# Masking half the key chunks on GpSimd after the exp, and moving three wide expert tiles

## The chip, the cores and the metric

The kernel runs on one core of one Trainium2 chip. The metric is the device time of one execution in microseconds; before the change the median of three runs is 723.05 us (722.39 to 724.26). The engines of a core run side by side and meet at semaphores: TensorE (PE) multiplies matrices, VectorE (DVE) and ScalarE (ACT) do elementwise work, GpSimd (POOL) does elementwise work and gathers, SyncE (SP) issues most transfers.

## The reference

Block-sparse attention over 4 batches of 8 heads, 768 positions, head size 64, in blocks of 32; then one expert of eight per token.

```python
scores = scale * np.matmul(q, k.transpose(0, 1, 3, 2))
mask = np.abs(blk_i - blk_j) <= 1                       # neighbouring blocks
mask |= (blk_i == 0) | (blk_j == 0) | (blk_i == n_blocks - 1) | (blk_j == n_blocks - 1)
for qb in range(n_blocks):
    for kb in sampled_blocks[qb]:                       # three random blocks for each
        mask[qb*32:(qb+1)*32, kb*32:(kb+1)*32] = True
scores = np.where(mask, scores, -1e9)
attn = softmax(scores)                                  # cut: minus max, exp, sum + 1e-9
x = (attn @ v)                                          # rows of 512: one per token, 3072 tokens
logits = x @ w_gate
expert_idx = argmax(logits); gate_w = softmax(logits)[expert_idx]
y = relu(x @ w1[expert_idx]) @ w2[expert_idx]           # w1: 512x1024, w2: 1024x512 for each expert
return gate_w[:, None] * y
```

The mask is the same for every head.

## The kernel before

Two stages. The attention goes through 16 pairs of heads (four batches of four pairs), each in two halves of 384 queries. Keys stand in six chunks of 128 on the partitions. For each chunk the scores of both heads go to one PSUM tile, ScalarE takes the exp, VectorE adds the six exps for the denominators, TensorE multiplies with v. There are three PSUM buffers for scores (`ps_s`, used by transposes too), and eight slots for exps (`ea`).

The mask is added to the scores by a second matmul into the same PSUM: `oh` (one-hot of a key's block) times `pen` (0 where a query sees the block, -2^33 where not), both bf16.

```python
def e_slot(n, half, c):
    return ea[:, ((2 * n + half) * NCH + c) % 8, :].rearrange("p (h q) -> p h q", h=2)

def scores(n, half, c):
    ...
    s = upper["ps_s"].tile([P, 2, 512], F32, name="s")
    for hh in range(2):
        r = slice(hh * D, (hh + 1) * D)
        nc.tensor.matmul(s[:, hh, :CW], lhsT=kT[r, c * P : (c + 1) * P], rhs=qT[r, cols], start=True, stop=False)   # L237
    for hh in range(2):
        r = slice(hh * D, (hh + 1) * D)
        nc.tensor.matmul(s[:, hh, :CW], lhsT=oh[r, c, :], rhs=pen[r, cols], start=False, stop=True)                 # L240
    e = e_slot(n, half, c)
    nc.scalar.activation(e, s[:, :, :CW], AF.Exp, scale=scale)                                                      # L242
    es[(n, half, c)] = e
    if c == 1:
        esums[(n, half)] = work.tile([P, 2, CW], F32, name="esum")
    if c > 0:
        t = esums[(n, half)]
        nc.vector.tensor_add(t[:], es[(n, half, 0)] if c == 1 else t[:], e)                                         # L248

def attend(n, half, c):
    ...
    for hh in range(2):
        nc.tensor.matmul(
            op[hh * D : (hh + 1) * D, :], lhsT=v_sb[:, hh, c, :], rhs=e[:, hh, :], start=(c == 0), stop=(c == NCH - 1),
        )                                                                                                           # L258
    ...

def divide(n, half):
    ...                                                             # sp: sums over keys, by TensorE, L271; ss: its copy
    for m in range(HC):
        nc.vector.reciprocal(r[:, m * P : (m + 1) * P], ss[:, m * P : (m + 1) * P])                                 # L278
    nc.vector.tensor_mul(oT[:], oT[:], r[:])                                                                        # L279

steps = [(n, half) for n in range(len(pairs)) for half in range(2)]
for i, (n, half) in enumerate(steps):
    ...
    if 0 < i and n + 1 < len(pairs):
        turn(*pairs[n + 1], half)                                   # tp: transposes of the next pair's k or q, L217
    for c in range(NCH):
        scores(n, half, c)
    if i == 0:
        make_mix()
    if i == 10:
        route_consts()                                              # small constants, on GpSimd
    if i > 0:
        divide(*steps[i - 1])
    for c in range(NCH):
        attend(n, half, c)
    if i == 0:
        turn(*pairs[1], 0)
    if n > 0:
        rows_out(n - 1, half)                                       # xr: rows of x and logits, L291; gate(b) at a batch's end
```

PE, DVE and POOL run their instructions in this order. `gate(b)` takes the softmax of a batch's logits and has one exp on ScalarE.

The experts' stage goes through 19 tiles of 128 tokens of one expert (`layer1`, L806; `layer2`, L820). For what is left of an expert there are three units (up to 224 tokens, L924 and L932) and three small tiles (32 tokens); unit u and small tile u stand behind tile `AT[u]`. Each tile, unit and small tile loads its expert's w1 and w2, 2 MB each, into two buffers for w1 and two for w2.

```python
AT = (8, 11, 14)
AT_S = (8, 11, 14)
...
for i in range(NS):
    ...
    if i + 3 in AT:
        gather_u(AT.index(i + 3))
    if i + 3 in AT_S:
        gather_s(AT_S.index(i + 3))
    if i + 2 in AT:
        turn_u()
    ...
    if i + 1 in AT:
        ...                                                         # layer 2 of tile i, the unit, layer 2 of tile i + 1
        layers_u(u, P + more * STEP, banks)
```

Of the kernel before, what the change touches and what calls it, by code (L numbers as in the profile page):

```python
# [17 lines left out]
def kernel(  # L18
# [30 lines left out]
    QR = 3 * P // 4  # L49
    STEP = P // 8  # L50
    MW = P + QR
    AT = (8, 11, 14)
    KU = len(AT)

    QS = P // 4
    AT_S = (8, 11, 14)
    KS = len(AT_S)
    NS = KA - -(N - KA * P - KU * MW - KS * QS) // P
    NTB = NC - KA
    NB_ = NTB + 2 * KU + KS  # L60
    assert KA < AT[0] - 2 and all(b - a > 2 for a, b in zip(AT, AT[1:])) and AT_S == AT and AT[-1] < NS - 3
    assert TA * P - E * (P - 1) > (KA - 1) * P
    XW = DM + 8
    scale = 1.0 / float(D) ** 0.5
# [56 lines left out]

    oh = mpool.tile([P, NCH, P], BF16, name="oh")
    pen = mpool.tile([P, S], BF16, name="pen")

    mix = mpool.tile([P, NPR, P + E], F32, name="mix")
    ones = mpool.tile([P, D], F32, name="ones")
# [61 lines left out]
    def make_mix():  # L188
        nc.scalar.dma_start(wg[:], moe_w_gate.rearrange("(c p) e -> p c e", p=P))
        nc.gpsimd.memset(mix[:], 0.0)  # L190
        for pr in range(NPR):
            nc.gpsimd.tensor_copy(mix[:, pr, :P], ident[:])
            nc.gpsimd.tensor_copy(mix[:, pr, P:], wg[:, pr, :])

    make_mask_pool = ExitStack()
    by_hand = ExitStack()
    by_hand.enter_context(tc.manual_schedule(engines={mybir.EngineType.Pool, mybir.EngineType.PE, mybir.EngineType.DVE}))
# [31 lines left out]
    def scores(n, half, c):  # L229

        b, pr = pairs[n]
        kT, qT = turned[(b, pr)][0], turned[(b, pr)][1]
        cols = slice(half * CW, (half + 1) * CW)
        s = upper["ps_s"].tile([P, 2, 512], F32, name="s")
        for hh in range(2):
            r = slice(hh * D, (hh + 1) * D)
            nc.tensor.matmul(s[:, hh, :CW], lhsT=kT[r, c * P : (c + 1) * P], rhs=qT[r, cols], start=True, stop=False)  # L237
        for hh in range(2):
            r = slice(hh * D, (hh + 1) * D)
            nc.tensor.matmul(s[:, hh, :CW], lhsT=oh[r, c, :], rhs=pen[r, cols], start=False, stop=True)  # L240
        e = e_slot(n, half, c)
        nc.scalar.activation(e, s[:, :, :CW], AF.Exp, scale=scale)  # L242
        es[(n, half, c)] = e
        if c == 1:
            esums[(n, half)] = work.tile([P, 2, CW], F32, name="esum")
        if c > 0:
            t = esums[(n, half)]
            nc.vector.tensor_add(t[:], es[(n, half, 0)] if c == 1 else t[:], e)  # L248

    def attend(n, half, c):  # L250
        v_sb = loaded[pairs[n]][2]
        if c == 0:

            ops_[(n, half)] = rt["bank"] = ps_o.tile([P, 512], F32, name="op")
        op = ops_[(n, half)][:, :CW]
        e = es[(n, half, c)]
        for hh in range(2):
            nc.tensor.matmul(  # L258
                op[hh * D : (hh + 1) * D, :], lhsT=v_sb[:, hh, c, :], rhs=e[:, hh, :], start=(c == 0), stop=(c == NCH - 1),
            )  # L260
        if c == NCH - 1:
            oT = work.tile([P, CW], F32, name="oT", bufs=3)
            nc.scalar.copy(oT[:], op)  # L263
            ops_[(n, half)] = oT
# [13 lines left out]
            nc.vector.reciprocal(r[:, m * P : (m + 1) * P], ss[:, m * P : (m + 1) * P])  # L278
        nc.vector.tensor_mul(oT[:], oT[:], r[:])  # L279

    def rows_out(n, half):

        b, pr = pairs[n]
        oT = ops_.pop((n, half))
        M = P + E
        xr = ps_x.tile([P, HC, M], F32, name="xr")

        M_ = D if n + 1 < len(pairs) else P
        for m in range(HC):
            for j in range(P // M_):  # L290
                nc.tensor.matmul(  # L291
                    xr[j * M_ : (j + 1) * M_, m, :], lhsT=oT[:, m * P + j * M_ : m * P + (j + 1) * M_], rhs=mix[:, pr, :],
                    start=True, stop=True,
                )
        if half == 0:
            xbs[n] = xpool.tile([P, NCH, M], F32, name="xb")
        xb = xbs[n]
        ms = slice(half * HC, (half + 1) * HC)
        nc.scalar.copy(xb[:, ms, :], xr[:])
        sofar = lgn[:, b * NCH + half * HC : b * NCH + (half + 1) * HC, :]  # L300
        if pr == 0:
            nc.vector.tensor_copy(sofar, xb[:, ms, P:])
        else:
            nc.vector.tensor_add(sofar, sofar, xb[:, ms, P:])
        if half == 1:
            rows = x_d[b * S : (b + 1) * S, pr * P : (pr + 1) * P]
            nc.sync.dma_start(rows.rearrange("(p c) w -> p c w", p=P), xb[:, :, :P])
            if pr == NPR - 1:
                gate(b)

    def gate(b):
        ts = slice(b * NCH, (b + 1) * NCH)
        nc.vector.reduce_max(lmax[:, ts], lgn[:, ts, :], axis=AX)
        ge = small.tile([P, NCH, E], F32, name="ge", bufs=2)
        nc.vector.tensor_tensor(
            ge[:], lgn[:, ts, :], lmax[:, ts].unsqueeze(2).to_broadcast([P, NCH, E]), op=ALU.subtract,
        )
        nc.scalar.activation(ge[:], ge[:], AF.Exp)
        gs = small.tile([P, NCH], F32, name="gs", bufs=2)
        nc.vector.reduce_sum(gs[:], ge[:], axis=AX)  # L320
        nc.vector.tensor_scalar_add(gs[:], gs[:], 1e-9)
        nc.vector.reciprocal(gs[:], gs[:])
        gw = small.tile([P, NCH, XW - DM], F32, name="gw", bufs=2)
        nc.vector.tensor_copy(gw[:], gs[:].unsqueeze(2).to_broadcast([P, NCH, XW - DM]))
        nc.sync.dma_start(x_d[b * S : (b + 1) * S, DM:].rearrange("(p c) w -> p c w", p=P), gw[:])

    pairs = [(b, pr) for b in range(B) for pr in range(NPR)]

    def shifted(n, half):

# [33 lines left out]
    def attention_again():  # L364
        for n in range(len(pairs)):
            load(*pairs[n])
            for which in range(2):
                turn(*pairs[n], which)
            for half in range(2):
                shifted(n, half)  # L370
                for c in range(NCH):
                    attend(n, half, c)
                divide(n, half)
                rows_out(n, half)

    def judge():

# [295 lines left out]
    def one_hots_1(ph, sl, T, n):  # L673
        sl_i = sm.tile([P, T], I32, name="sl_i" + ph)
        nc.vector.tensor_copy(sl_i[:], sl[:])
        rc_i = sm.tile([P, 2, T], I32, name="rc_i" + ph)
        nc.vector.tensor_scalar(rc_i[:, 0, :], sl_i[:], scalar1=P - 1, scalar2=None, op0=ALU.bitwise_and)
        nc.vector.tensor_scalar(rc_i[:, 1, :], sl_i[:], scalar1=7, scalar2=None, op0=ALU.arith_shift_right)
        rc = rt["rc" + ph] = sm.tile([P, 2, T], F32, name="rc" + ph)
        nc.vector.tensor_copy(rc[:], rc_i[:])  # L680
        oc = sm.tile([P, T, n], BF16, name="oc" + ph)
        nc.vector.tensor_tensor(
            oc[:], rt["iota_r"][:, None, :n].to_broadcast([P, T, n]), rc[:, 1, :].unsqueeze(2).to_broadcast([P, T, n]),
            op=ALU.is_equal,
        )
        tk = rt["tk" + ph] = sm.tile([P, T, 2, n], BF16, name="tk" + ph)
        for j in range(2):
            nc.vector.tensor_tensor(  # L688
                tk[:, :, j, :], oc[:], rt["tok"][:, j, :T].unsqueeze(2).to_broadcast([P, T, n]), op=ALU.mult,
            )  # L690
        rt["or" + ph] = sm.tile([P, T, P], BF16, name="or" + ph)

    def tokens(ph, T, n):

# [258 lines left out]


    steps = [(n, half) for n in range(len(pairs)) for half in range(2)]
    NA = (B - 1) * NPR
    load(*pairs[1])
    for i, (n, half) in enumerate(steps):
        if half == 1 and n + 2 < len(pairs):
            load(*pairs[n + 2])  # L960
        if 0 < i and n + 1 < len(pairs):
            turn(*pairs[n + 1], half)
        for c in range(NCH):
            scores(n, half, c)
        if i == 0:
            make_mix()
        if i == 10:
            route_consts()
        if i > 0:
            divide(*steps[i - 1])  # L970
        for c in range(NCH):
            attend(n, half, c)
        if i == 0:
            turn(*pairs[1], 0)
        if n > 0:
            rows_out(n - 1, half)

        if (n, half) == (NA, 1):
            ranks("A", 0, TA)
        if (n, half) == (NA + 1, 0):  # L980
            count("A")
            layout_a()
            for i_ in range(2):
                fetch(i_, 1)
                fetch(i_, 2)
        if (n, half) == (NA + 1, 1):
            slots_a()
        if n == NA + 2:
            one_hots("A", rt["slA"], TA, KA, half)
        if (n, half) == (NA + 3, 0):  # L990
            tokens("A", TA, KA)
            for i_ in range(3):
                gather(i_)
        if n + 1 == len(pairs) and half == 1:
            turn_x(0)
# [6 lines left out]
    for i in range(NS):  # L1002
# [58 lines left out]
        if i == 1:  # L1061
            tokens("B", NT, NB_)
        if i == 2:
            judge()
        if i == 4:
            tokens_s()
        if i == 3:
            for u in range(KU):
                at = rt["xeU"][0:1, KU + u : KU + u + 1]
# [96 lines left out]
```

## Time and profile before

The profiled execution has a span of 722.3 us. One half of a pair is about 10.8 us, and the attention takes the first 355 us; the experts' stage takes the rest.

| engine | busy us | share of the span | instructions |
|---|---|---|---|
| TensorE | 701.8 | 97% | 5134 |
| VectorE | 393.6 | 54% | 825 |
| ScalarE | 281.2 | 39% | 456 |
| GpSimd | 72.6 | 10% | 114 |

An average over both stages hides that their limits differ: VectorE is busy 70 to 80% of most of the attention and little later, the transfers are the other way round (25% to 36% of the DMA engines' time in most of the attention, mostly 88% and more from 370 us on). In the lines that follow, a line of the order of time has start, length, engine, line of the kernel, operation, output and inputs, shape, and number of instructions put together; in square brackets stands the idle time before it. A line of a group has count, busy time and mean length, then the idle time before it and who ended it. One matmul of f32 stands as two records.

### The profile page before, as it was taken

What the parts mean: (1) busy time and instruction counts of PE and PEld (TensorE: products, weight loads), DVE (VectorE), ACT (ScalarE), POOL (GpSimd) and SP (SyncE); (2) the same over time, 40 slices, a digit from 0 to 9 for tenths busy, and PEclk for the clock granted to TensorE, in tenths of its full rate; (3) what the DMA queues carried; (4) which work ended last, traced back from release to release, by engine and by line L of the source; (5) the groups of instructions that cost most, each with busy time, mean ns of one, the idle gap of its engine ahead of it and who ended that gap; (6) DMA issues with size and microseconds to landing.
All of it is one profiled execution on the core that took longest, in us unless ns stands there. A gap on an engine that the chain in (4) does not pass through costs nothing.

```text
span 722.3 us, 13053 instructions
## 1 busy us (share of the span) xinstructions
PE 701.8 (97%) x5134; PEld 457.6 (63%) x5134; DVE 393.6 (54%) x825; ACT 281.2 (39%) x456; POOL 72.6 (10%) x114
## 2 busy tenths in 40 slices
PE   8999999999999999999999999999999999899993
PEld 5555555555555555555677776778787868677861
DVE  6677778678678678999748025820227011902200
ACT  3756756756756766765411110111111111111110
POOL 7000000000000000000202112201130013011210
PEclk9999999999999999999999999999999999999998
DMA  9312323322333322193278899996999399979950
GB/s 198 88 50 62 88 74 84 89 60 51 89 81 76 88 65 47 47 382 129 82 256 289 309 321 362 360 333 222 378 395 370 147 364 396 399 237 384 397 188 18
DMA packets 114566, 145.48 MB, mean 201 GB/s; under 512 B 56227, under 2 KB 72675, under 8 KB 114468
## 3 DMA queue, kind: packets, MB, share of 16 engines
q1 hardware_dynamic: 107968, 129.84, 54.1%
q0 software_dynamic: 4368, 14.02, 5.1%
q8 instruction: 51, 0.84, 0.5%
q10 hardware_dynamic: 2132, 0.41, 0.3%
q14 instruction: 47, 0.39, 0.2%
HBM read 131.47 MB, written 12.94 MB: 200 GB/s over the span
## 4 chain that ended last, share of the span: by engine, by line
PE 57%; issue 33%; POOL 4%; DVE 3%; DMA 1%; POOLq 0%; ACTq 0%; another core or an unknown queue 0%; DVEq 0%
PE s L237 17%; PE op L258 17%; PE hp L806 6%; PE s L240 4%; PE sp L271 4%; PE xr L291 3%; PE zp L820 3%; PE tp L217 2%; POOL out_dram L835 2%; POOL xg L738 1%; DMA q_sb<-in_q_dram 1%; DVE orB L668 0%; POOL ea L858 0%; POOL ea L903 0%; DVE tkB L688 0%
## 5 line engine op out<-in xcount | busy, mean ns | idle before, releaser
L237 PE MATMUL s<-qT,kT 64*128 64x384 f32 x768 | 157.1, 487 | 1.2 <-DVE qT L222 1.2
L242 ACT ACTIVATE ea<-s 128x768 f32<-128x768 f32 x192 | 152.3, 813 | 6.2 <-PE s L240 4.2
L806 PEld LDWEIGHTS hp<-xgT,w 128*128 128x128 f32 x1216 | 138.3, 192 | 7.8 <-issue 5.1
L806 PE MATMUL hp<-xgT,w 128*128 128x128 f32 x1216 | 140.7, 276 | 1.4 <-ACT hT L813 1.4
L787 DVE STREAM_TRANSPOSE xgT<-xg 32x128 f32<-32x128 f32 x208 | 62.9, 302 | 128.6 <-PE hp L806 98.8
L248 DVE TENSOR_TENSOR esum<-esum,ea 128x768 f32<-128x768 f32 x128 | 122.7, 958 | 13.8 <-ACT ea L242 0.5
L258 PE MATMUL op<-ea,v_sb 128*64 128x384 f32 x768 | 129.3, 486 | 0.0
L820 PE MATMUL zp<-w,hT 128*128 128x512 f32 x256 | 112.7, 594 | 0.0
L258 PEld LDWEIGHTS op<-ea,v_sb 128*64 128x64 f32 x768 | 55.1, 137 | 68.8 <-issue 68.8
L237 PEld LDWEIGHTS s<-qT,kT 64*128 64x128 f32 x768 | 66.4, 187 | 37.6 <-issue 34.4
L278 DVE RECIPROCAL r<-ss 128x128 f32<-128x128 f32 x96 | 82.2, 912 | 1.3 <-ACT ss L273 1.3
L820 PEld LDWEIGHTS zp<-w,hT 128*128 128x128 f32 x256 | 47.5, 190 | 54.6 <-issue 54.6
L813 ACT ACTIVATE hT<-hp 128x512 f32<-128x512 f32 x36 | 21.5, 597 | 114.3 <-PE hp L806 106.4
L248 DVE TENSOR_TENSOR esum<-ea 128x768 f32<-128x768 f32 x32 | 30.7, 958 | 59.8 <-ACT ea L242 59.8
L240 PE MATMUL s<-pen,oh 64*128 64x384 bf16 x384 | 62.9, 322 | 0.0
L263 ACT COPY oT<-op 128x384 f32<-128x384 f32 x32 | 15.3, 479 | 106.2 <-PE op L258 106.2
L825 ACT ACTIVATE zo<-zp,xg 128x512 f32<-128x512 f32 x16 | 11.0, 687 | 101.7 <-PE zp L820 101.7
L913 DVE STREAM_TRANSPOSE ea<-ea 32x128 f32<-32x128 f32 x84 | 21.7, 285 | 29.7 <-DMA ea<-x_rows,gB 29.0
L240 PEld LDWEIGHTS <-oh 64*128 64x128 bf16 x384 | 19.0, 94 | 25.1
L291 PEld LDWEIGHTS xr<-mix,oT 128*64 128x64 f32 (+1 forms) x372 | 24.1, 139 | 10.7 <-issue 10.7
L835 POOL DMA_INDIRECT out_dram<-zo,sB x14 | 14.0, 1004 | 167.2 <-ACT zo L825 119.1
L738 POOL DMA_INDIRECT xg<-x_rows,gA x5 | 6.1, 1224 | 220.7 <-ACT ea L242 219.4
(278 smaller groups left out, 520.2 us busy)
## 6 DMA issues: line engine op xcount, KB each, us to landing
w<-in_moe_w_dram SPq DMA_DIRECT2D x50, 2048.0 KB
k_sb<-in_k_dram SPq DMA_DIRECT2D x32, 192.0 KB
v_sb<-in_v_dram SPq DMA_DIRECT2D x16, 384.0 KB
x_rows<-xb SPq DMA_DIRECT2D x16, 384.0 KB
q_sb<-in_q_dram SPq DMA_DIRECT2D x30, 192.0 KB
sums<-ss SPq DMA_DIRECT2D x32, 3.0 KB
q_sb<-in_q_dram ACTq DMA_DIRECT2D x2, 192.0 KB
xg<-x_rows,gB POOLq DMA_INDIRECT x15, 7.0
```

The costliest lines, as they stand in the source:

```text
L237: nc.tensor.matmul(s[:, hh, :CW], lhsT=kT[r, c * P : (c + 1) * P], rhs=qT[r, cols], start=True, stop=False)
L240: nc.tensor.matmul(s[:, hh, :CW], lhsT=oh[r, c, :], rhs=pen[r, cols], start=False, stop=True)
L242: nc.scalar.activation(e, s[:, :, :CW], AF.Exp, scale=scale)
L248: nc.vector.tensor_add(t[:], es[(n, half, 0)] if c == 1 else t[:], e)
L258: nc.tensor.matmul(op[hh * D : (hh + 1) * D, :], lhsT=v_sb[:, hh, c, :], rhs=e[:, hh, :], start=(c == 0), stop=(c == NCH - 1),)
L271: nc.tensor.matmul(sp[hh * D : (hh + 1) * D, :], lhsT=ones[:], rhs=esum[:, hh, :], start=True, stop=True)
L278: nc.vector.reciprocal(r[:, m * P : (m + 1) * P], ss[:, m * P : (m + 1) * P])
L291: nc.tensor.matmul(xr[j * M_ : (j + 1) * M_, m, :], lhsT=oT[:, m * P + j * M_ : m * P + (j + 1) * M_], rhs=mix[:, pr, :], start=True, stop ...
L787: nc.vector.transpose(xT[d, :, t], xg[t, :DM].rearrange("p (c q) -> p c q", c=DB)[:, :, d])
L806: nc.tensor.matmul(hp[:, m, :], lhsT=st[i]["w1"][:, c, fb * P : (fb + 1) * P], rhs=st[i]["xT"][:, c, :], start=(c == 0), stop=(c == DB - 1),)
L820: nc.tensor.matmul(zp[:], lhsT=st[i]["hT"][:, fb, :], rhs=st[i]["w2"][:, fb, :], start=(fb == 0), stop=(fb == FB - 1),)
L835: ins = nc.gpsimd.indirect_dma_start(out=to[:, :], out_offset=bass.IndirectOffsetOnAxis(ap=at, axis=0), in_=rows, in_offset=None, bounds_c ...
```

## The change

- In pairs 1 to 11 (the first three batches without the first pair) chunks 0, 1 and 2 have no mask matmul. Instead GpSimd multiplies their exps in place with a 0/1 mask in SBUF (bf16, three chunks of 128x768), which is made once behind the first half by six matmuls and three compares.
- The chunks are multiplied with v in the order 3, 0, 4, 1, 5, 2, and VectorE's adds start behind the fourth exp, so that GpSimd has time before a masked chunk is read.
- The exp of `gate(b)` and what follows it come after the next half's products with v; the route constants are made in half 0, since GpSimd is taken later.
- Units and small tiles stand behind tiles 6, 10 and 14, four tiles apart.

```diff
-    AT = (8, 11, 14)
+    AT = (6, 10, 14)
...
-    AT_S = (8, 11, 14)
+    AT_S = (6, 10, 14)
...
+    LATE = (0, 1, 2)
+    ORDER = (3, 0, 4, 1, 5, 2)
+    mask = mpool.tile([P, len(LATE), S], BF16, name="mask")
...
+    def make_late():
+        for j, c in enumerate(LATE):
+            bm = upper["ps_s"].tile([P, 2, 512], F32, name="bm", tag="s")
+            for half in range(2):
+                cols = slice(half * CW, (half + 1) * CW)
+                nc.tensor.matmul(bm[:, half, :CW], lhsT=oh[:D, c, :], rhs=pen[:D, cols], start=True, stop=True)
+            nc.vector.tensor_single_scalar(mask[:, j, :].rearrange("p (h q) -> p h q", h=2), bm[:, :, :CW], 0.0, op=ALU.is_ge)
...
+        late = c in LATE and 0 < n < NA
...
-            nc.tensor.matmul(s[:, hh, :CW], lhsT=kT[r, c * P : (c + 1) * P], rhs=qT[r, cols], start=True, stop=False)
-        for hh in range(2):
+            nc.tensor.matmul(s[:, hh, :CW], lhsT=kT[r, c * P : (c + 1) * P], rhs=qT[r, cols], start=True, stop=late)
+        for hh in range(0 if late else 2):
             r = slice(hh * D, (hh + 1) * D)
             nc.tensor.matmul(s[:, hh, :CW], lhsT=oh[r, c, :], rhs=pen[r, cols], start=False, stop=True)
...
-        if c == 1:
-            esums[(n, half)] = work.tile([P, 2, CW], F32, name="esum")
-        if c > 0:
+        if late:
+            m = mask[:, LATE.index(c), cols]
+            nc.gpsimd.tensor_tensor(e, e, m[:, None, :].to_broadcast([P, 2, CW]), op=ALU.mult)
+        if c >= 3:
+            if c == 3:
+                esums[(n, half)] = work.tile([P, 2, CW], F32, name="esum")
             t = esums[(n, half)]
-            nc.vector.tensor_add(t[:], es[(n, half, 0)] if c == 1 else t[:], e)
+            for c_ in {3: (0,), 4: (4, 1), 5: (5, 2)}[c]:
+                nc.vector.tensor_add(t[:], es[(n, half, 3)] if c == 3 else t[:], es[(n, half, c_)])
...
         if i == 0:
             make_mix()
-        if i == 10:
             route_consts()
         if i > 0:
             divide(*steps[i - 1])
-        for c in range(NCH):
+        for c in ORDER:
             attend(n, half, c)
         if i == 0:
+            make_late()
             turn(*pairs[1], 0)
+        if "gates" in rt:
+            gate_weights(*rt.pop("gates"))
```

Cut: `gate` is split into its first part and `gate_weights`, `tokens_s` comes two tiles earlier, and the one-hot tiles of the two routings share a buffer.

More of the change, by code (lines that the diff above doesn't have):

```diff
@@ L60 @@
     NB_ = NTB + 2 * KU + KS
-    assert KA < AT[0] - 2 and all(b - a > 2 for a, b in zip(AT, AT[1:])) and AT_S == AT and AT[-1] < NS - 3
+    assert KA < AT[0] and all(b - a > 2 for a, b in zip(AT, AT[1:])) and AT_S == AT and AT[-1] < NS - 3
     assert TA * P - E * (P - 1) > (KA - 1) * P
@@ L123 @@
     pen = mpool.tile([P, S], BF16, name="pen")
+    LATE = (0, 1, 2)
+    ORDER = (3, 0, 4, 1, 5, 2)
+    assert NCH == 6
+    mask = mpool.tile([P, len(LATE), S], BF16, name="mask")
     mix = mpool.tile([P, NPR, P + E], F32, name="mix")
@@ L243, in scores @@
         es[(n, half, c)] = e
-        if c == 1:
-            esums[(n, half)] = work.tile([P, 2, CW], F32, name="esum")
-        if c > 0:
+        if late:
[4 more added lines that the diff above has]
+                esums[(n, half)] = work.tile([P, 2, CW], F32, name="esum")
             t = esums[(n, half)]
-            nc.vector.tensor_add(t[:], es[(n, half, 0)] if c == 1 else t[:], e)
+            for c_ in {3: (0,), 4: (4, 1), 5: (5, 2)}[c]:
+                nc.vector.tensor_add(t[:], es[(n, half, 3)] if c == 3 else t[:], es[(n, half, c_)])
     def attend(n, half, c):
         v_sb = loaded[pairs[n]][2]
-        if c == 0:
+        if c == ORDER[0]:
             ops_[(n, half)] = rt["bank"] = ps_o.tile([P, 512], F32, name="op")
@@ L258, in attend @@
             nc.tensor.matmul(
-                op[hh * D : (hh + 1) * D, :], lhsT=v_sb[:, hh, c, :], rhs=e[:, hh, :], start=(c == 0), stop=(c == NCH - 1),
+                op[hh * D : (hh + 1) * D, :], lhsT=v_sb[:, hh, c, :], rhs=e[:, hh, :], start=(c == ORDER[0]), stop=(c == ORDER[-1]),
             )
-        if c == NCH - 1:
+        if c == ORDER[-1]:
             oT = work.tile([P, CW], F32, name="oT", bufs=3)
@@ L279, in divide, with rows_out @@
         nc.vector.tensor_mul(oT[:], oT[:], r[:])
-    def rows_out(n, half):
+    def rows_out(n, half, again=None):
         b, pr = pairs[n]
@@ L308, in rows_out, with gate @@
             if pr == NPR - 1:
-                gate(b)
-    def gate(b):
+                gate(b, again)
+    def gate(b, n_again=None):
         ts = slice(b * NCH, (b + 1) * NCH)
@@ L317, in gate, with gate_weights @@
         )
+        if b < B - 1 and n_again is None:
+            rt["gates"] = (b, ge)
+        else:
+            gate_weights(b, ge)
+    def gate_weights(b, ge):
         nc.scalar.activation(ge[:], ge[:], AF.Exp)
@@ L327 @@
     pairs = [(b, pr) for b in range(B) for pr in range(NPR)]
+    NA = (B - 1) * NPR
     def shifted(n, half):
@@ L370, in attention_again @@
                 shifted(n, half)
-                for c in range(NCH):
+                for c in ORDER:
                     attend(n, half, c)
                 divide(n, half)
-                rows_out(n, half)
+                rows_out(n, half, True)
     def judge():
@@ L690, in one_hots_1 @@
             )
-        rt["or" + ph] = sm.tile([P, T, P], BF16, name="or" + ph)
+        rt["or" + ph] = sm.tile([P, T, P], BF16, name="or" + ph, tag="or")
     def tokens(ph, T, n):
@@ L955 @@
     steps = [(n, half) for n in range(len(pairs)) for half in range(2)]
-    NA = (B - 1) * NPR
     load(*pairs[1])
@@ L970 @@
             divide(*steps[i - 1])
-        for c in range(NCH):
+        for c in ORDER:
             attend(n, half, c)
         if i == 0:
+            make_late()
             turn(*pairs[1], 0)
+        if "gates" in rt:
+            gate_weights(*rt.pop("gates"))
         if n > 0:
@@ L1063 @@
         if i == 2:
+            tokens_s()
             judge()
-        if i == 4:
-            tokens_s()
         if i == 3:
```

## The prediction

> **What bounds the kernel now.** I read the page first: engine shares, then the 40 slices. Columns of the first line are busy us (share of the span) and number of instructions; a digit of the second is the busy tenths of one slice of 18 us.
>
> ```profile
> PE 701.8 (97%) x5134; PEld 457.6 (63%) x5134; DVE 393.6 (54%) x825; ACT 281.2 (39%) x456; POOL 72.6 (10%) x114
> ...
> PE   8999999999999999999999999999999999899993
> ...
> DVE  6677778678678678999748025820227011902200
> ...
> POOL 7000000000000000000202112201130013011210
> ```
>
> TensorE has work from beginning to end, and GpSimd next to none in the attention (slices 2 to 19). A busy matmul row says little by itself, because matmuls overlap; so I went to the order of time on TensorE in one half of a pair (start, length, what):
>
> ```profile
> 153.38 0.81 PE L237 MATMUL s<-qT,kT 64*128 64x384 f32 x4
> 154.03 0.33 PE L240 MATMUL s<-pen,oh 64*128 64x384 bf16 x2
> 154.28 0.87 PE L271 MATMUL sp<-esum,ones 128*64 128x384 f32 x4
> 154.98 4.04 PE L258 MATMUL op<-ea,v_sb 128*64 128x384 f32 x24
> 158.85 0.86 PE L291 MATMUL xr<-mix,oT 128*64 128x136 f32 x12
> 159.65 0.59 PE L217 MATMUL tp<-ident,k_sb 64*128 64x64 f32 x12
> 160.07 0.86 PE L237 MATMUL s<-qT,kT 64*128 64x384 f32 x4
> 160.77 0.33 PE L240 MATMUL s<-pen,oh 64*128 64x384 bf16 x2
> 160.93 0.81 PE L237 MATMUL s<-qT,kT 64*128 64x384 f32 x4
> ```
>
> Starts follow one another without a hole and no line carries an idle time: the attention is paced by TensorE. From the starts, one chunk of scores is 0.65 us of L237 and 0.16 us of L240 (160.77 to 160.93). The two L240 matmuls of a chunk are each 0.33 us long, yet together take the place of 0.16 us. The first exp of a half starts at 150.36 and of the next at 161.14 in ScalarE's order of time, so a half lasts **10.78 us**. Six chunks at 0.81 us, sp 0.70, op 3.87, xr 0.80 and tp 0.42 are 10.65 of it.
>
> In the second stage I asked for TensorE's waits after 340 us (us in total, times, longest):
>
> ```profile
> PE hpu L924 <- DMA w<-in_moe_w_dram: 3.9, 2, 2.3
> PE hp L806 <- ACT hT L813: 1.4, 3, 0.5
> ```
>
> The first are the units behind tiles 11 and 14, whose first weights come 1.65 and 2.25 us late; the unit behind tile 8 waits for nothing.
>
> The other engines, from the groups (busy us, mean ns of one):
>
> ```profile
> L242 ACT ACTIVATE ea<-s 128x768 f32<-128x768 f32 x192 | 152.3, 813 | 6.2 <-PE s L240 4.2
> ...
> L248 DVE TENSOR_TENSOR esum<-esum,ea 128x768 f32<-128x768 f32 x128 | 122.7, 958 | 13.8 <-ACT ea L242 0.5
> ...
> L278 DVE RECIPROCAL r<-ss 128x128 f32<-128x128 f32 x96 | 82.2, 912 | 1.3 <-ACT ss L273 1.3
> ```
>
> A half costs VectorE five adds (4.8), three reciprocals (2.57 by the order of time), one oT product (0.56) and one logit add (0.18), 8.1 us of 10.78. ScalarE has six exps (4.85) and copies, about 7.2. Neither is the bound.
>
> [...] in the first 17 us, in GpSimd's and VectorE's order of time:
>
> ```profile
> 12.99 0.24 POOL L424 TENSOR_SCALAR past<-row 128x1 f32<-128x1 f32 x1
> 13.32 0.19 POOL L425 TENSOR_TENSOR quarter<-quarter,past 128x1 f32<-128x1 f32 x1
> ...
> 14.62 0.97 POOL L425 TENSOR_TENSOR quarter<-quarter,past 128x1 f32<-128x1 f32 x1
> ```
>
> ```profile
> 3.93 2.67 DVE L169 SCALAR_TENSOR_TENSOR allow<-kb,samp,allow 24x24 f32<-24x24 f32 x3
> ...
> 14.58 4.15 DVE L248 TENSOR_TENSOR esum<-esum,ea 128x768 f32<-128x768 f32 x4
> ```
>
> The same one-element GpSimd op takes 0.19 us alone and 0.97 us beside an esum add that started at 14.58; and three 24-element VectorE ops take 0.89 us each while GpSimd's selects of 768 elements (0.86 us each) run. It is a lock, in both directions. [...] No run here shows a long two-input GpSimd op. [...]
>
> **The change part by part.**
>
> 1. *Mask matmuls removed.* Chunks 0, 1, 2 in pairs 1 to 11, two halves: 66 chunks. 66 x 0.16 = **-10.7 us** of TensorE, or 0.48 us a half: TensorE's own pace becomes 10.30 us. TensorE being the bound, this counts in full if nothing else takes over.
>
> 2. *GpSimd products added.* 66 products, 128x768 f32 times a bf16 mask, three a half. [...] TensorE does not wait for them either: in the half above the first exp ends at 151.17, [...] in the order 3, 0, 4, 1, 5, 2 the last masked chunk is read at about 157.7 (154.98 less 0.48 of removed matmuls, plus five chunks of 0.645).
>
> 3. *The lock.* What excludes one another in a half is VectorE's five adds, oT product and logit add, 5 x 0.96 + 0.56 + 0.18 = 5.52 us, and three products of length T: 5.52 + 3T. [...] So the lock equals the old pace at T = 1.75 and frees the new pace of 10.30 only at T below 1.59. Over 22 halves: -10.7 us for T up to 1.59, [...] +16 us at 2.0 (11.52).
>
> 4. *The mask made ahead* (half 0). Six bf16 matmuls and three VectorE compares of 128x768 from PSUM. A 128x384 copy from PSUM takes 0.55 us here (L222), so a compare of twice that is some 0.95. VectorE's five adds now start behind the fourth exp (about 15.2 us) and end near 20.4; compares end near 21.5, 22.5 and 23.5. The three score buffers hold the compares' input, so the next tp, tp and first score matmuls, which stood at 19.81, 20.23 and 20.61, wait one after the other: the first score starts near 23.5. **+2.9 us**.
>
> 5. *Units at 6, 10, 14.* Four tiles, not three, between units. A tile is 14.0 us of TensorE (452.24 to 466.25) and asks for two loads of 2 MB; with a unit and its small tile come four more loads in a burst. After the unit behind 8 the DMA share is 0.92 to 1.04 from 500 to 560 us, a backlog that three tiles don't work off. A fourth adds 14.0 us against two loads at 5.3 us each (the shortest distance between landings, from the packets) and about 1.4 us of gathers and stores: 2 us to spare, as much as the larger wait. Both waits go: **-3.9 us**. Before tile 6 TensorE waits for no load, so an earlier first unit is safe.
>
> 6. *Gates' exp one half later, constants in half 0, adds behind the fourth exp.* TensorE waits for none of these before, and what they do is not on its path: 0.
>
> Sum of 1, 4 and 5 with a free lock: -10.7 + 2.9 - 3.9 = -11.7, or 711. [...]
>
> **The rivals.** *The lock takes over* (T of 1.7 or more): for it, the 0.97 us above [...]. It gives 718 to 740. Against it, [...] one-input GpSimd work here runs at a rate that a two-input loop of 2 reads an element would do in 2 x 0.83 x 768 = 1.28 us plus 0.19, 1.47 us (the copies of 128 and 8 columns, 291 and 192 ns, give 0.83 ns an element). *The late masked chunks stall TensorE through the eight exp buffers*: the fifth add of a half ends later than before, and the fifth exp of the next half writes the buffer it reads. Unblocked there are some 5 us between them, so it only joins in when the lock already binds, and would add 1 to 3 us. *The loads stay late*: the burst, not the spacing, sets them, and the waits only move: 4 us less gain, 715 with a free lock.
>
> **Range and chances.** I take T from 1.45 to 1.8 as about equally likely and weigh the free lock a little more than half, because even 1.47 us follows from this trace's own rates. That puts the middle at 715. The low end is the full sum and a few us of small gains, 709; the high end is T near 1.95, 734. Over 2% faster (below 708.6) needs more than TensorE gives up: 0.06. Over 2% slower (above 737.5) needs T of 2.0 or more: 0.12. Within 2%: 0.82.
>
> **What would show it.** The L255 group (mask matmuls) has 252 rows and not 384. A product's time by itself, when no add stands beside it, should be 1.4 to 1.8 us; adds beside products should be longer than 958 ns by the wait for the lock. The distance of exps between halves should be 10.3 us with a free lock; 10.6 to 11 with holes in TensorE that end on GpSimd or VectorE says the lock binds. The first score of half 1 near 23.5 us shows step 4. No wait for weights before the units shows step 5. It is wrong if TensorE waits for the products though the lock is free, or if a unit behind tile 6 meets loads that have not caught up.

## The result, and the profile after

The changed kernel takes **733.54 us** (median of four runs, 733.36 to 736.21) against 722.96 us: a ratio of **1.0152**, 95% interval 1.0126 to 1.0179. It is 1.5% slower. The prediction was 715 us, 1.1% faster than before, with 709 to 734 as the range: the time is just inside the range, the direction is wrong. That it lies inside is luck: the high end stood for a GpSimd product of about 1.95 us, and the product takes 1.64.

The page of the changed kernel; the same lines as of before:

```profile
PE 697.8 (95%) x5008; PEld 455.3 (62%) x5008; DVE 440.4 (60%) x828; ACT 271.8 (37%) x456; POOL 184.0 (25%) x180
...
PE   8999997999979999999999899999999998999994
...
DVE  5799997999979998899747109302660027402200
...
POOL 6145544445535430000202211021210222011210
```

TensorE is busy 4 us less and the kernel takes 9.5 us longer. TensorE's string has dips in slices 7, 12 and 23 (7, 7 and 8), where it was full before: holes in single places, not a slower pace. VectorE is nearly full in the attention, and GpSimd is at work there now.

The groups of the instructions that the change added or touched (busy us, mean ns), the last two of them first as they were before the change:

```profile
L279 DVE TENSOR_TENSOR oT<-oT,r 128x384 f32<-128x384 f32 x32 | 17.9, 558 | 1.1
L304 DVE TENSOR_TENSOR lgn<-lgn,xb 128x24 f32<-128x24 f32 x24 | 4.4, 182 | 5.8 <-ACT xb L299 5.8
```

```profile
L261 POOL TENSOR_TENSOR ea<-ea,mask 128x768 f32<-128x768 f32 x66 | 115.3, 1775 | 131.7 <-ACT ea L257 118.4 <-DVE r L297 13.2
...
L298 DVE TENSOR_TENSOR oT<-oT,r 128x384 f32<-128x384 f32 x32 | 31.6, 986 | 1.1
...
L323 DVE TENSOR_TENSOR lgn<-lgn,xb 128x24 f32<-128x24 f32 x24 | 23.1, 962 | 5.3 <-ACT xb L318 5.3
```

The lock can be read here although no line names it: a logit add of 24 columns takes 962 ns and took 182 before, an oT product 986 and took 558. That is waiting, written down as work. A GpSimd product takes 1636 ns at the least (the shortest of the 66).

TensorE in an ordinary half of the changed kernel, in order of time:

```profile
161.91 0.59 PE L231 MATMUL tp<-ident,k_sb 64*128 64x64 f32 x12
162.33 2.80 PE L252 MATMUL s<-qT,kT 64*128 64x384 f32 x16
164.97 0.32 PE L255 MATMUL s<-pen,oh 64*128 64x384 bf16 x2
...
166.84 0.87 PE L290 MATMUL sp<-esum,ones 128*64 128x384 f32 x4
167.53 4.04 PE L277 MATMUL op<-ea,v_sb 128*64 128x384 f32 x24
171.40 0.86 PE L310 MATMUL xr<-mix,oT 128*64 128x136 f32 x12
172.20 0.59 PE L231 MATMUL tp<-ident,q_sb 64*128 64x64 f32 x12
```

No hole, and from one tp to the next 10.29 us: the predicted pace, to 0.01 us. So the loss lies elsewhere. TensorE's waits show where (us in total, times, longest):

```profile
PE s L252 <- ACT ea L257: 9.6, 3, 4.4
PE hp L833 <- DMA w<-in_moe_w_dram: 3.9, 2, 2.0
PE okp L417 <- DVE okn L416: 3.3, 2, 2.6
```

The first line stands at the end of each of three batches (4.43, 4.43 and 0.71 us). ScalarE at the first of them:

```profile
105.73 4.51 ACT L257 ACTIVATE ea<-s 128x768 f32<-128x768 f32 x6
...
120.64 0.24 ACT L344 ACTIVATE ge<-ge 128x48 f32<-128x48 f32 x1 [4.53 <-DVE ge L334]
120.79 2.19 ACT L257 ACTIVATE ea<-s 128x768 f32<-128x768 f32 x3
```

and VectorE and TensorE beside it:

```profile
110.21 1.63 DVE L323 TENSOR_TENSOR lgn<-lgn,xb 128x24 f32<-128x24 f32 x1
111.76 0.95 DVE L267 TENSOR_TENSOR esum<-ea 128x768 f32<-128x768 f32 x1
...
120.40 0.21 DVE L334 TENSOR_TENSOR ge<-lgn,lmax 128x48 f32<-128x48 f32 x1
```

```profile
115.05 2.15 PE L252 MATMUL s<-qT,kT 64*128 64x384 f32 x12
121.64 1.65 PE L252 MATMUL s<-qT,kT 64*128 64x384 f32 x4 [4.43 <-ACT ea L257]
```

The exp of the gates is **ahead** of the next half's six exps in ScalarE's queue. The text of the changed kernel has it behind them, but only PE, DVE and POOL keep the order of the text here; ScalarE's is chosen by the scheduler, which took the gates' exp first. It waits 4.53 us for VectorE's `ge`, the exps wait behind it, the three score buffers fill, and TensorE stops after three chunks. Before the change the exp stood ahead of the next exps too, and cost next to nothing there, since VectorE delivered in time:

```profile
107.22 4.85 ACT L242 ACTIVATE ea<-s 128x768 f32<-128x768 f32 x6
...
117.85 0.24 ACT L318 ACTIVATE ge<-ge 128x48 f32<-128x48 f32 x1 [0.24 <-DVE ge L315]
```

In all four batches together it waited 1.4 us before and 11.1 us now.

Where the 9.5 us between the two profiled spans (722.3 and 731.8) come from, by the start of the first exp of each half:

| part | working | us |
|---|---|---|
| mask made ahead | pair 1 starts at 33.68, not 31.76; the first half itself started 0.3 us earlier here | +1.9 |
| pace of 22 halves | 22 x (10.29 - 10.78) | -10.8 |
| two batch ends | (15.06 + 11.63) + (15.06 + 11.78) - 4 x 10.29 | +12.4 |
| third batch end, and the rest of the attention | last half at 349.15, not 344.37, less the lines above | +1.3 |
| experts' stage | 372.75 us behind the last sp matmul, not 367.97 | +4.8 |

The pace paid what it was to pay, and two kinds of wait took more than that. (The parts are rounded; they sum to 9.6.)

### The profile page after: what moved, and what is told of

Read it like the earlier page. It is cut to its first block, busy times and chain, and to the rows that moved or that the text cites. A ratio compares the mean times of both kernels' runs of the same rounds, so it can differ in the third digit from the quotient of the medians.

```text
span 731.8 us, 12893 instructions
## 1 busy us (share of the span) xinstructions
PE 697.8 (95%) x5008; PEld 455.3 (62%) x5008; DVE 440.4 (60%) x828; ACT 271.8 (37%) x456; POOL 184.0 (25%) x180
## 4 chain that ended last, share of the span: by engine, by line
issue 40%; DVE 28%; PE 22%; POOL 4%; DMA 2%; ACT 1%; POOLq 0%; DVEq 0%; ACTq 0%; another core or an unknown queue 0%
DVE esum L267 13%; PE s L252 8%; PE op L277 7%; DVE r L297 6%; DVE lgn L323 2%; POOL out_dram L862 2%; PE hp L833 2%; POOL xg L765 2%; PE sp L290 2%; PE s L255 2%; PE xr L310 1%; ACT ea L257 1%; DVE ea L940 1%; DMA xg<-x_rows,gB 1%; PE tp L231 1%
## 5 line engine op out<-in xcount | busy, mean ns | idle before, releaser
L252 PE MATMUL s<-qT,kT 64*128 64x384 f32 x768 | 149.6, 496 | 10.9 <-ACT ea L257 9.6
L257 ACT ACTIVATE ea<-s 128x768 f32<-128x768 f32 x192 | 146.0, 812 | 9.3 <-PE s L255 6.9
L261 POOL TENSOR_TENSOR ea<-ea,mask 128x768 f32<-128x768 f32 x66 | 115.3, 1775 | 131.7 <-ACT ea L257 118.4
L833 PE MATMUL hp<-xgT,w 128*128 128x128 f32 x1216 | 142.3, 278 | 5.3 <-DMA w<-in_moe_w_dram 3.9
L267 DVE TENSOR_TENSOR esum<-esum,ea 128x768 f32<-128x768 f32 x128 | 126.2, 986 | 12.2 <-ACT ea L257 0.5
L252 PEld LDWEIGHTS s<-qT,kT 64*128 64x128 f32 x768 | 68.4, 190 | 52.5 <-ACT ea L257 28.7
L267 DVE TENSOR_TENSOR esum<-ea 128x768 f32<-128x768 f32 x32 | 37.4, 1169 | 22.2 <-ACT ea L257 22.1
L255 PE MATMUL s<-pen,oh 64*128 64x384 bf16 x252 | 41.7, 326 | 0.0
L298 DVE TENSOR_TENSOR oT<-oT,r 128x384 f32<-128x384 f32 x32 | 31.6, 986 | 1.1
L290 PE MATMUL sp<-esum,ones 128*64 128x384 f32 x128 | 27.7, 512 | 0.0
```

Of the source, the lines that this page charges most:

```text
L261: nc.gpsimd.tensor_tensor(e, e, m[:, None, :].to_broadcast([P, 2, CW]), op=ALU.mult)
L267: nc.vector.tensor_add(t[:], es[(n, half, 3)] if c == 3 else t[:], es[(n, half, c_)])
L290: nc.tensor.matmul(sp[hh * D : (hh + 1) * D, :], lhsT=ones[:], rhs=esum[:, hh, :], start=True, stop=True)
L833: nc.tensor.matmul(hp[:, m, :], lhsT=st[i]["w1"][:, c, fb * P : (fb + 1) * P], rhs=st[i]["xT"][:, c, :], start=(c == 0), stop=(c == DB - 1),)
```

## The experiments

Times are compared with the kernel before on the same chip, whose median in the first four was 724.4 us, in the second four 724.17 and in the last 723.13.

**1. The gates' exp truly behind the next half's exps.**

```diff
-            nc.scalar.copy(oT[:], op)
+            rt["copied"] = nc.scalar.copy(oT[:], op)
...
     def gate_weights(b, ge):
-        nc.scalar.activation(ge[:], ge[:], AF.Exp)
+        with tc.issue_after(getattr(rt["copied"], "ins", rt["copied"])):
+            nc.scalar.activation(ge[:], ge[:], AF.Exp)
```

> The changed kernel with one thing different: on ScalarE the exp of the gates is queued behind the next half's copy of the product with v, and so behind its six exps, where the change put it only in the text. Theory (ScalarE, which runs in order, stands behind the gates' exp, which waits for VectorE): the two halves of 15.06 us become 10.29, the ones after them 10.3 instead of 11.63 and 11.78, the half of 12.16 about 11; 733.5 - 2 x 6.2 - 1 = 720, +-1.5. Rival (VectorE is behind because of the lock with GpSimd, and will catch up with TensorE at some other point): halves beyond 10.3 stay, 728 or more.

Measured: 720.49 us, ratio 0.9941 (0.9921 to 0.9961). From the changed kernel's 1.0152 that is 2.1%, 15 us (the two intervals leave about 2.5 us either way). All halves of pairs 1 to 11 but the last are now 10.29 or 10.30 us, the batch ends too; from the first exp of pair 1 to that of the last half it is 302.07 us instead of 315.47, and the 13.4 us of difference are the two batch ends' 12.4 and 1.0 of the third batch end and the halves behind it. (Pair 1 starts at 35.73 in this profile and not at 33.68, mostly because the first score chunks of the kernel started 1.6 to 1.7 us apart instead of 0.81. Such a start is no part of the change; the kernel of experiment 9 has it too, so halves and stages are compared and not whole spans.) ScalarE's queue shows the mend, in the kernel of experiment 3:

```profile
118.70 3.65 ACT L257 ACTIVATE ea<-s 128x768 f32<-128x768 f32 x5
...
127.02 0.48 ACT L282 COPY oT<-op 128x384 f32<-128x384 f32 x1 [3.14 <-PE op L277]
127.40 0.24 ACT L345 ACTIVATE ge<-ge 128x48 f32<-128x48 f32 x1
```

The rival, that VectorE's lag would come out elsewhere, falls: in most halves VectorE's first add starts 6.0 to 7.0 us behind the half's first exp, where it was mostly 6.0 in the changed kernel. It lags no less, and the halves still keep 10.29.

**2. The health check ahead of the small tiles' row lists.**

```diff
         if i == 2:
-            tokens_s()
             judge()
+            tokens_s()
```

> The changed kernel with one thing different: behind tile 2 the health check (judge) comes ahead of the small tiles' row lists (tokens_s), as it did before the change. Theory (VectorE stands in order behind a result of TensorE for the row lists, TensorE then waits 3.3 us for the health check and runs at half its clock for a while): 3.3 us of wait and 1.6 us of slower matmuls go, 728.5 +-1. Rival (the wait is there because the route lists came late, and moves elsewhere): 732 to 734.

Measured: 730.57 us, ratio 1.0088 (1.007 to 1.0106), 0.64% or 4.6 us below the changed kernel. From the last half's first exp to the end of the profile it is 377.1 us, where it is 382.7 in the changed kernel and 377.9 in the kernel before. The changed kernel's VectorE explains it:

```profile
400.27 0.20 DVE L734 TENSOR_TENSOR sB<-tvB,noneB 128x35 int32<-128x35 f32 x1
414.16 0.16 DVE L742 COPY tvS<-tps 128x3 f32<-128x3 f32 x1 [13.69 <-PE tps L740]
...
416.10 0.55 DVE L416 TENSOR_REDUCE okn<-ok 64x1 f32<-64x384 f32 x1
```

VectorE has nothing to do from 400.5 to 414 because the copy at the head of its queue waits for TensorE, and the sums for the health check, whose inputs are long there, stand behind the copy. When TensorE comes to the check, it has to wait for them:

```profile
416.70 0.19 PE L417 MATMUL okp<-ones,okn 64*1 64x1 f32 x2 [2.58 <-DVE okn L416]
417.64 0.19 PE L417 MATMUL okp<-ones,okn 128*1 128x1 f32 x2 [0.76 <-DVE okn L416]
417.76 5.47 PE L833 MATMUL hp<-xgT,w 128*128 128x128 f32 x32
```

3.34 us of wait, and 32 matmuls that start over 5.31 us and not 3.68, at a granted clock of 0.50 from 418.7 to 420.7 us and of 1.00 from 421.7. In the order of experiment 2 the sums are made by 405.9 us, and TensorE goes through:

```profile
416.81 0.30 PE L417 MATMUL okp<-ones,okn 64*1 64x1 f32 x4
```

**3. Both mends.** The two diffs together.

> Both of the two mends together. Theory: they lie in different stages and add up, 733.5 - 13.4 - 5 = 715 +-2, which is below the kernel before (723). Rival: one of them uncovers another wait, 720 or more.

Measured: **715.49 us, ratio 0.9871 (0.9854 to 0.9888)**: 1.3% faster than the kernel before, and the sum of the two single gains (0.9941 - 0.0064 = 0.9877). This version is faster than both kernels.

**4. Both mends, units at 8, 11 and 14 again.**

```diff
-    AT = (6, 10, 14)
+    AT = (8, 11, 14)
-    AT_S = (6, 10, 14)
+    AT_S = (8, 11, 14)
```

> Both mends, and units and small tiles behind tiles 8, 11 and 14 again. Theory (the burst of loads at a unit and its small tile sets the late weights, not the distance of the next unit): the same time as with 6, 10 and 14, within 1 us. Rival (the distance of four tiles pays, as predicted): 3 to 4 us slower.

Measured: 716.47 us, ratio 0.9894 (0.9871 to 0.9917). The interval overlaps that of experiment 3; a gain of four tiles' distance can be 1 us and is not 4 (see experiment 9). From the last half's first exp to the end the two profiles differ by 0.2 us (377.6 here, 377.7 in experiment 3).

**5. The exp not put off.**

```diff
-        if b < B - 1 and n_again is None:
-            rt["gates"] = (b, ge)
-        else:
-            gate_weights(b, ge)
+        gate_weights(b, ge)
```

> The changed kernel with the exp of the gates not put off (its place in the text as before the change). Theory (VectorE's lateness makes the wait, wherever the text has the exp, as long as ScalarE has it ahead of the next exps): the exp stands between two copies of kT, the long halves stay at 15 us or a little more, 733 to 735. Rival (putting it off made the wait): 10.8 us or less for these halves, 720 to 722.

Measured: 735.89 us, ratio 1.0163 (1.0127 to 1.02). The two long halves are 15.42 and 15.41 us. So putting the exp off didn't make the wait; put off in the text or not, it stood ahead of the exps in the queue, and what had changed is when VectorE delivers.

**6. No products.** Chunks 0, 1 and 2 of pairs 1 to 11 stay unmasked here, which changes the routing too, so only the attention's halves are read.

```diff
-            nc.gpsimd.tensor_tensor(e, e, m[:, None, :].to_broadcast([P, 2, CW]), op=ALU.mult)
```

> The changed kernel without GpSimd's products: chunks 0, 1 and 2 of pairs 1 to 11 stay unmasked, so only the attention's halves are compared. Theory (VectorE is late for two reasons, its adds now start behind the fourth exp, 3.3 us, and the oT product and logit add wait for GpSimd, 1.1 us): ScalarE still waits about 3.4 us for the gates at each of two batch ends, halves of about 13.7. Rival (the lock alone makes VectorE late): no wait, 10.3 to 10.8. Other halves 10.29 in both, as with the products.

Measured: ordinary halves 10.29 us as with the products, batch ends 11.85 us. My split was wrong. VectorE at the first batch end before the change, then VectorE and ScalarE at the same place without products:

```profile
108.87 0.96 DVE L248 TENSOR_TENSOR esum<-ea 128x768 f32<-128x768 f32 x1 [2.31 <-ACT ea L242]
```

```profile
110.67 0.96 DVE L266 TENSOR_TENSOR esum<-ea 128x768 f32<-128x768 f32 x1 [2.05 <-ACT ea L257]
```

```profile
107.72 4.51 ACT L257 ACTIVATE ea<-s 128x768 f32<-128x768 f32 x6
...
119.43 0.24 ACT L343 ACTIVATE ge<-ge 128x48 f32<-128x48 f32 x1 [1.32 <-DVE ge L333]
```

The first add comes 1.65 us after the half's first exp before the change (108.87 and 107.22), 2.95 without products (110.67 and 107.72), and 6.03 with them (111.76 and 105.73). So 1.3 us of VectorE's lag are the adds' new place behind the fourth exp, and 3.1 are the products. That these act through the lock, and not by an add that waits for a product's result, is read from the trace: VectorE has no idle time ahead of the add at 111.76, its logit add lasts 1.63 us instead. ScalarE's wait follows: 0.24, 1.32 and 4.53 us. A batch end costs 1.5 us without products (11.85 + 10.23 less 2 x 10.29) and 6.1 to 6.3 with them. The rival that the lock does it alone is nearer than what I held, and not the whole either.

**7. Two chunks masked on GpSimd, with both mends.**

```diff
-    LATE = (0, 1, 2)
+    LATE = (0, 1)
```

> Both mends, but only chunks 0 and 1 masked on GpSimd. Theory (TensorE is the pace with three products, the lock costs nothing): 10.29 + 0.16 = 10.45 us a half, 22 x 0.16 = 3.5 us slower than three chunks, 719. Rival (the lock already takes time with three): same or faster, 713 to 715.

Measured: 717.71 us, ratio 0.9911 (0.9892 to 0.993), every half of pairs 1 to 11 but the last 10.45 us. From the first exp of pair 1 to that of the last half it is 305.51 us, and 302.00 in experiment 3: the third chunk pays its 0.16 us a half in full, and with three products TensorE is still the pace. (The medians are only 2.2 us apart; their intervals are wide enough for 3.5.)

**8. Four chunks, with both mends.** Chunk 5 takes the mask of chunk 0 (`LATE.index(c) % 3`; the expectation says the third chunk's, which makes no difference to the time), so again only the halves are read. The mask tile keeps its three chunks.

```diff
-    LATE = (0, 1, 2)
-    ORDER = (3, 0, 4, 1, 5, 2)
+    LATE = (0, 1, 2, 5)
+    ORDER = (3, 0, 4, 1, 2, 5)
...
-            m = mask[:, LATE.index(c), cols]
+            m = mask[:, LATE.index(c) % 3, cols]
-            for c_ in {3: (0,), 4: (4, 1), 5: (5, 2)}[c]:
+            for c_ in {3: (0,), 4: (4, 1), 5: (2, 5)}[c]:
```

> Both mends, and chunk 5 masked on GpSimd too, by the third chunk's mask for want of space, so only the attention's halves are compared. Theory (lock: three products and five adds already fill 5.17 + 5.12 = 10.29 us): four products of 1.72 and the adds are 12.0 us a half, with TensorE standing idle. Rival (the lock does not bind): TensorE's pace, 10.29 - 0.16 = 10.13 us.

Measured: most halves 11.35 to 11.96 us, 11.44 the usual one, where three products give 10.29 and TensorE alone would give 10.13. TensorE with four products, and its total wait for them:

```profile
153.60 0.87 PE L290 MATMUL sp<-esum,ones 128*64 128x384 f32 x4 [0.59 <-DVE esum L267]
154.29 3.40 PE L277 MATMUL op<-ea,v_sb 128*64 128x384 f32 x20
158.63 0.87 PE L277 MATMUL op<-ea,v_sb 128*64 128x384 f32 x4 [0.94 <-POOL ea L261]
```

```profile
PE op L277 <- POOL ea L261: 21.3, 22, 1.4
```

Now it waits for the product of the last chunk, in each of 22 halves. GpSimd and VectorE together are the bound: four products of 1.64 and five adds of 0.96 that exclude each other are 11.36 us. The expected 12.0 us was too much by half a microsecond.

**9. The unit positions alone, on the kernel before.**

```diff
-    AT = (8, 11, 14)                     # AT_S likewise; the assert on AT[0] is relaxed
+    AT = (6, 10, 14)
...
         if i == 2:
             judge()
-        if i == 4:
             tokens_s()
```

> The kernel before with units and small tiles behind tiles 6, 10 and 14, and the row lists of the small tiles made behind the health check of tile 2; nothing else of the change. Theory (the burst of loads sets the late weights, which then stand ahead of a plain tile): within 1.5 us of before. Rival (four tiles of distance pay the 3.9 us that were predicted): 3 to 4 us faster.

Measured over fourteen runs: 723.85 us, ratio 1.0006 (0.9994 to 1.0018). No gain.

## Why the prediction was wrong

*Step 1, mask matmuls*, was right: 10.78 to 10.29 us a half, -10.8 us, in the trace and by the sum; experiment 7 shows the same 0.16 us a chunk.

*Step 2, the product's length*, was right: 1.64 us when it runs undisturbed, between the 1.47 estimated from this trace's own rates (copies of 128 and 8 columns, 291 and 192 ns) and the upper end of 1.8, which was the author's own estimate.

*Step 3, the lock*, had the right kind of wait and a threshold that was a little too strict: its terms sum to 5.54 (not 5.52), with 3 x 1.64 to 10.46 us, and yet 10.29 was kept. GpSimd in one half:

```profile
106.62 5.17 POOL L261 TENSOR_TENSOR ea<-ea,mask 128x768 f32<-128x768 f32 x3 [5.12 <-ACT ea L257]
```

VectorE's oT product gets its turn among the three products, which take 5.17 us with it and not 3 x 1.64 + 0.56; the five adds lie in the 5.12 us in between. The margin is small: in the profile of experiment 3 VectorE's first add starts 6.62, 6.51, 6.41, 6.31 and 6.20 us behind the half's first exp in five successive halves, so VectorE gains 0.1 us a half, and the lock by itself would allow about 10.2 us (an estimate from these). Experiment 8 shows that it does bind with one more product. The wait is shown by this, by the logit add's 962 ns and by experiment 6. The reciprocals, which the step's sum leaves out, ran beside the products without it: three take 2.57 us from 106.58, beside a product that starts at 106.62, and took 2.57 before. What the step left out is what the lock does *below* its threshold: it cost no throughput (10.29 us a half), but VectorE's adds start 3.1 us later in most halves, and with only two products (experiment 7) still 1.5 us later (4.41 against 2.95 behind the first exp). The step asked only whether the pace would hold.

*Step 4, the mask ahead*, was right in kind: +1.9 us, not +2.9, or 2.3 without the 0.3 us by which this first half started earlier. VectorE's adds began at 14.79, not 15.2, and the compares follow each other by 0.87 us, not by 1.0.

*Step 5, the units*, was wrong: 0, not -3.9. With three tiles between, the late load was the next unit's; with four it is that of the plain tile ahead of the unit, and the waits are 1.89 and 2.02 us there. The first of them, before and after:

```profile
549.47 6.29 PE L924 MATMUL hpu<-ea,w 128*128 128x224 f32 x32 [1.65 <-DMA w<-in_moe_w_dram]
```

```profile
531.42 7.38 PE L833 MATMUL hp<-xgT,w 128*128 128x128 f32 x64 [1.89 <-DMA w<-in_moe_w_dram]
```

Both stand at the same distance behind the unit before them (69.2 us from its start at 480.26, 69.5 from 461.97), which fits the third rival: the burst of loads at a unit and its small tile sets what comes late, not the spacing. In the other profiles the waits for weights lie between 0.3 and 4.1 us in all, with the same positions too, so they are no firm quantity.

***Step 6 is the step that failed*: "TensorE waits for none of these before, and what they do is not on its path: 0."** The adds behind the fourth exp, and more so the lock of step 3, make VectorE late (1.3 and 3.1 us), and the gates' exp, which the step took to be one half later because the text said so, stood ahead of the next exps in ScalarE's queue and waited for VectorE: +12.4 us at two batch ends and +1.0 behind them (experiment 1). A second cost is in no step: the row lists of the small tiles, which the change puts ahead of the health check in VectorE's queue: +4.8 us by the table, 4.6 by experiment 2. Neither cost is a matter of how much work an engine has; both are of the order in a queue.

The sum with these is -10.8 + 1.9 + 13.4 + 4.8 = +9.3, and 9.5 was measured between the profiles. Without the two queue orders the change does about what was predicted for it with a free lock, less the units: -11.7 + 3.9 is -7.8 us, or the third rival's 715, and experiment 3 measured 715.49, 9 us below the kernel before (8 to 11 by its interval).

## What to carry to other kernels

VectorE was off the path here and still held up ScalarE's queue, by 4.53 us at a batch end: before moving work between engines, list for each in-order queue what stands ahead of the operations on the path and whether its input comes later now. The place of the gates' exp in the text, behind the next half's six exps, was not its place in ScalarE's queue, which is not kept by hand in this kernel; look at the queue itself. And when two engines wait for each other's instructions, ask how much later each result comes (3.1 us here) as well as whether the pace holds (10.29 us a half, as predicted).

## What the runs showed of the hardware

The stop of 4.43 us cost TensorE more than 4.43 us here. The windows of the changed kernel around the first batch end (busy us and count of each engine, granted clock, DMA):

```profile
119.00:121.60 2.60, 0.00 (x0) 0.00 (x0) 1.51 (x5) 0.96 (x3) 0.00 (x0) 0.90 0.38 86
121.60:123.40 1.80, 1.76 (x7) 0.98 (x9) 0.00 (x0) 1.39 (x2) 1.74 (x2) 0.50 0.00 0
123.40:126.00 2.60, 2.60 (x16) 1.14 (x16) 1.22 (x2) 1.78 (x3) 2.60 (x2) 0.79 0.01 3
```

The granted clock (the third number from the end) is 0.50 for the first matmuls after the stop: the first four take 1.44 us from their start to the next, where 0.65 is usual, and the clock is whole again only after some 3 us: 0.50 until 124 us, 0.75 from 124 to 125, 1.00 from there (0.79 is the mean of the last line). The half with TensorE's wait of 4.43 us is 4.8 us longer, and the next one, in which these matmuls lie, 1.3 us longer (1.5 at the second batch end). After the health check, where TensorE had 0.36 us of work in 3.7 us, the clock was 0.58 for the 2.3 us that followed.

A wait for the lock shows in this trace as busy time of the instruction that waits, on either engine, and no line of the waits names it: the logit add's mean goes from 182 to 962 ns, and a product's is 1775 ns where the shortest takes 1636. The change of a small instruction's mean length is where it was to be seen.
